# A planned kernel for hashed attention and two expert layers: wider zero products, a later start of a head's transposes, and a new planned order

## The chip, the cores and the metric

One core of one Trainium2 chip. The metric is the device time of one execution in microseconds; the median of several executions counts. The kernel before takes 838.75 us (three runs, 838.18 to 839.08).

## The reference

Only the numbers of the work matter here, and what depends on what.

```python
# q, k, v: (2, 8, 768, 64); proj: (64, 6)
bucket = sum over 6 bits of (x @ proj > 0) * 2**bit         # for q and for k
scores = where(q_bucket == k_bucket, q @ k.T / 8, -1e9)     # 16 heads of 768 x 768
attn   = softmax(scores);  y = attn @ v                     # -> x: (1536, 512)
g      = h * tanh(softplus(h)),  h = x @ w_in               # 512 -> 2048
x2     = g @ w_out                                          # 2048 -> 512
out    = ((x2 @ w1) * (x2 @ w2)) @ w3 @ w_out2              # 512 -> 1024 -> 1024 -> 512
```

## The kernel before, in words

Everything is computed in float32 accuracy: a float32 operand is split into a high and a low part in the type fp32r, and three products of the parts (`PASS`) stand for one. The sixteen heads are worked through one after the other. **A head** (`prep`, `scores`, `unit`, `values`, `norm`): its q and k are split and transposed on TensorE (L441, into a PSUM pair `s`), copied out by ScalarE as `qb` and `kb` (L447), the hash bits are products with `psel` (L472) and are compared on VectorE (L479, L484); then come six score tiles of 128 rows (L499, four products each, into `s`), each with its maximum on VectorE (L508) and its exponential on ScalarE (L511); the exponentials `E` are transposed on TensorE (L545, three to a bank `b`), copied out as `T` by ScalarE or VectorE (L400), and multiplied with v (L569). At the head's end the six sums are inverted (L522 to L524), transposed (L528), copied as `rt` (L530) and stored to `r_d`. There are two pairs `s` and four banks `b` in PSUM.

**Weights**: raw weights (8-byte numbers) are loaded by GpSimd's queue (L622), decoded by one ScalarE operation and three VectorE operations (L606 to L615, on 128x1024 elements), and stored again as `keep_...` (L640). Later SyncE's queue fetches them (L654), and they are split (L661, L663). The product of w3 and w_out2 (`wprod`, L694, L711) is computed beside the heads, and so is the whole chain of the first block of 512 tokens (`ff_first`: L775, L791, L886), whose input is scaled with rows of `r_d` (`x_split`, L742 to L762). Its banks are evicted by ScalarE or VectorE (L821, L851, L895, L897, L922). The two other blocks of 512 tokens follow (L775, L1133, L1160, L1188).

**The order** is made by a planner (`Plan`). Each step is a `P.op`: an engine (or two to choose from), an assumed duration, what it reads and writes, and a due time. `Plan.run` goes forward in its own time: it finds the engine on which a step can begin first, and of the steps that can begin there then takes the one that is due first. A value (`Val`) gets a buffer of its pool when the first step that names it begins, and a kind of value may hold at most `lim` buffers. What a step hands on counts as there after its duration, a latency (`LAT`, or its own `lat`) and `slack`. Each engine then runs its steps in this order and waits on semaphores, so an assumed duration sets the order alone, not the waiting. `CFG` has the due times' parameters, in units of one score tile, the most ScalarE-only `T` copies (`tc`, in score tiles), and the most banks that the first block's chain may hold (`F`).

**Zero products**: after planning, `Plan.fill` goes through the gaps that the plan leaves on TensorE (up to `fill`, 60 of the plan's microseconds), and puts products of zeros (`zeros`, L392) into a bank that is free then. Their number is the gap's length divided by an assumed duration of one.

Of the kernel before, what the change touches and what calls it, by code (L numbers as in the profile page):

```python
# [24 lines left out]
PASS = ((0, 0), (0, 1), (1, 0))  # L25

CFG = {
    "lag": 1.18,
    "prep": 8.06,
    "wp0": 16.01,  # L30
    "wp1": 51.97,
    "dec0": 47.99,
    "dec1": 88.63,
    "ff0": 56.0,
    "ff1": 102.69,
    "slack": 0.10,
    "k8": 12,
    "f4": 7,
    "hl": 3,
    "F": 3,  # L40
    "cold": 8.0,
    "fill": 60.0,
    "tc": 22,
}


# [34 lines left out]


class Plan:
    LAT = {"PE": 0.22, "DVE": 0.17, "ACT": 0.17, "POOL": 0.3, "SP": 2.3, "SWAP": 0.0}

    def __init__(self):
        self.units = []
# [58 lines left out]
    def fill(self, order):  # L146

        last = 0.0
        for u in [x for x in order if x.eng == "PE"]:
            a, b = last, u.start  # L150
            last = u.start + u.alts["PE"]
            if a > CFG["fill"]:
                break
            n = int((b - a - 0.15) / 0.06)
            if n < 4:
                continue
            for p in self.filler_pools:
                for i in range(len(p.bufs)):
                    if all(y <= a or x >= b + 0.1 for x, y in p.spans.get(i, [])):
                        f = Unit()  # L160
                        f.alts, f.eng, f.start, f.idx, f.name = {"PE": b - a - 0.1}, "PE", a + 0.01, -1, "zero"
                        f.fn = lambda p=p, i=i, n=n: self.filler(p.bufs[i], n)
                        order.append(f)
                        p.spans.setdefault(i, []).append((a, b))
                        break
                else:
                    continue
                break
# [118 lines left out]
def kernel(  # L287
# [14 lines left out]
    nc = tc.nc  # L302
# [86 lines left out]
    def zeros(t, n):  # L389
        t = t[:, 0] if len(t.shape) == 3 else t  # L390
        for _ in range(n):
            nc.tensor.matmul(t[:, 0:128], lhsT=zr, rhs=zr, start=True, stop=True)  # L392

    P.filler, P.filler_pools = zeros, (BP, SP_)
    P.free["PE"] = 1.3
# [25 lines left out]
    def prep(u, d0, step):  # L421

        def d(x):
            return d0 + x * step

        qb, kb, qa, ka = feat[u] = Val(QB, "f"), Val(KB, "f"), Val(QA, "f"), Val(KA, "f")
        for x, (nm, hi, fb) in enumerate((("q", 0, qb), ("k", 1, kb))):
            raw = raws.pop((u, nm))
            hl = Val(HL, "h")
            P.op(EITHER, (act(C * D, True), dve2(C * D)), lambda e, raw=raw, hl=hl, hi=hi: copy(e, hl()[:, :, hi, :], raw()),  # L430
                 r=[raw], w=[(hl, "hi")], due=d(x), name=f"sp{u}")
            P.op("DVE", dve(C * D), lambda raw=raw, hl=hl, hi=hi: nc.vector.tensor_sub(
                out=hl()[:, :, 1 - hi, :], in0=raw(), in1=hl()[:, :, hi, :]),
                r=[raw, (hl, "hi")], w=[(hl, "lo")], due=d(x), name=f"sp{u}")
            t = Val(SP_, "tq", 1)

            def tr(hl=hl, t=t):
                tt = t().bitcast(FR)
                for c in range(C):
                    a, i = divmod(c, CH)  # L440
                    nc.tensor.transpose(  # L441
                        tt[:, a, i * 128:(i + 1) * 128], hl()[:, c].rearrange("p s d -> p (s d)"), identr)

            P.op("PE", 6 * 0.082, tr, r=[hl], w=[t], due=d(x + 1), name=f"tq{u}")

            def fbc(t=t, fb=fb, nm=nm):
                nc.scalar.activation(  # L447
                    out=fb().rearrange("p (a n) -> p a n", a=2), in_=t()[:, :, 0:HS], func=AF.Copy,
                    scale=1.0 if nm == "q" else 1.0 / float(D) ** 0.5)

            P.op("ACT", act(S) + 0.01, fbc, r=[t], w=[fb], due=d(x + 1.3), name=f"fb{u}")
        xf = None
        if u > 1:
            xf = Val(XF, "x")
            for sl, fb, nm in ((slice(0, D), qb, "q"), (slice(D, 2 * D), kb, "k")):
                P.op("SP", 0.5, lambda sl=sl, fb=fb: nc.sync.dma_start(
                    out=xf()[sl].bitcast(F32), in_=fb()[sl].bitcast(F32)), r=[fb], w=[(xf, nm)], due=d(2.5), lat=2.0, name=f"xf{u}")
        P.op(EITHER, (act(S, True), dve2(S)), lambda e: copy(e, qa()[0:D], qb()[0:D]),
             r=[qb], w=[(qa, "x")], due=d(2.2), name=f"fa{u}")
        P.op(EITHER, (act(S, True), dve2(S)), lambda e: copy(e, ka()[0:D], kb()[D:2 * D]),  # L460
             r=[kb], w=[(ka, "x")], due=d(3.2), name=f"fa{u}")
        t = Val(SP_, "tq", 1)

        def bits(a):
            cols = slice(a * HS, (a + 1) * HS)
            ops = [(psel[:, 0, 0, :], qb()), (psel[:, 1, 0, :], kb())]
            if xf is None:
                ops += [(psel[:, 0, 1, :], qb()), (psel[:, 1, 1, :], kb())]
            else:
                ops += [(psel2, xf())]  # L470
            for n, (w, f) in enumerate(ops):
                nc.tensor.matmul(t()[:, a, 0:HS], lhsT=w, rhs=f[:, cols], start=(n == 0), stop=(n == len(ops) - 1))  # L472

        for a in range(2):
            P.op("PE", pe(HS, 4 if xf is None else 3), lambda a=a: bits(a),
                 r=[qb, kb, v_psel] + ([xf, v_psel2] if xf else []), w=[(t, a)], due=d(4), name=f"bits{u}")

        def cmp():
            nc.vector.tensor_scalar(  # L479
                out=qa()[D:128].rearrange("p (a n) -> p a n", a=2), in0=t()[D:128, :, 0:HS],  # L480
                scalar1=ccol[D:128, 1:2], scalar2=ccol[D:128, 0:1], op0=ALU.is_le, op1=ALU.mult)

        P.op("DVE", 0.99, cmp, r=[t, v_ccol], w=[(qa, "m")], due=d(4.3), name=f"cmp{u}")
        P.op("DVE", dve2(S), lambda: nc.vector.tensor_copy(out=ka()[D:KR], in_=qa()[96:96 + 2 * NB]),  # L484
             r=[(qa, "m")], w=[(ka, "m")], due=d(4.6), name=f"km{u}")
# [30 lines left out]
    def norm(u, due):  # L516
# [3 lines left out]
        def sc():  # L520
# [10 lines left out]
             due=due + 0.6, name=f"nr{u}")  # L531
        P.op("SP", 0.5, lambda: nc.sync.dma_start(
            out=r_d[h % 2, h // 2, b * S:(b + 1) * S].rearrange("(c p) -> c p", p=128), in_=rt()),
            r=[rt], w=[(v_rd, (u, ))], due=due + 0.7, lat=2.2, name=f"rd{u}")

    def n0_of(u, a):
        return u * C + a * CH
# [81 lines left out]
    def rawload(src, due, nm, after=()):  # L619
        raw = Val(K8, "raw", 2, I32)  # L620
        m = src.shape[1]
        P.op("POOL", 1.0, lambda: nc.gpsimd.dma_start(  # L622
            out=raw().rearrange("p (m n) -> p m n", m=m), in_=src), w=[raw], due=due, lat=8.0, name=nm + "l", after=after)
        return raw

    WSRC = {"wi": w_in, "wo": w_out, "wa": w1, "wb": w2}
# [7 lines left out]
    def decode_chunk(nm, j, due, waits=None):  # L634
        raw = rawload(chunk_src(nm, j), due - 1.5, f"{nm}{j}", after=late_gate + (waits or []))
        g = Val(F4, "g", 2)
        decode(raw, g, due, f"{nm}{j}")
        keep[nm, j] = dram.tile([128, 1024], F32, tag=f"{nm}{j}", name=f"keep_{nm}{j}")
        kept[nm, j] = Val()
        P.op("POOL", 1.0, lambda: nc.gpsimd.dma_start(out=keep[nm, j], in_=g()), r=[g], w=[kept[nm, j]],  # L640
             due=due + 0.4, lat=4.5, name=f"{nm}{j}s")

    hl_lim, ld_lim, fx_lim, late, fetched = [CFG["hl"]], [2], [1], [""], []

    def fetch(nm, j, due, ahead, after=()):

        after = list(after) + fetched[-1:]
        f, hl = Val(F4, "ld" + late[0], ld_lim[0]), Val(K8, "hl" + late[0], hl_lim[0], FR)
        if nm == "wp":
            src = wp_d[j * 256:(j + 1) * 256].rearrange("(f p) d -> p f d", p=128)  # L650
            P.op("SP", 0.5, lambda: nc.sync.dma_start(out=f().rearrange("p (f d) -> p f d", f=2), in_=src),
                 r=[(v_wp, 2 * j), (v_wp, 2 * j + 1)], w=[f], due=due - ahead - 1, lat=4.0, after=after, name=f"{nm}{j}ld")
        else:
            P.op("SP", 0.5, lambda: nc.sync.dma_start(out=f(), in_=keep[nm, j]), r=[kept[nm, j]], w=[f],  # L654
                 due=due - ahead - 1, lat=4.0, after=after, name=f"{nm}{j}ld")
        fetched.append(P.units[-1])
        split(f, hl, due - ahead)
        return hl
# [72 lines left out]
    def x_split(n, due, after=()):  # L731
# [3 lines left out]
        for kk in range(KD):  # L735
# [5 lines left out]
            for e in range(2):  # L741
                P.op("SP", 0.5, lambda e=e, kk=kk, rb=rb: nc.sync.dma_start(  # L742
                    out=rb()[e * D:(e + 1) * D], in_=r_d[e, kk, t0:t1].partition_broadcast(D)),
                    r=[(v_rd, (x, )) for x in us if x % 2 == e], w=[(f, ("r", e)), (xh, ("a", kk, e))], due=due, lat=2.3,
                    after=after, name=f"rb{n}")
            need = [(X[n], (x, a)) for x in us for a in range(2)
                    if (x // H) * S + a * HS < t1 and (x // H) * S + (a + 1) * HS > t0]
# [461 lines left out]
    OPS = {"h": b_h, "out": b_out, "x2": b_x2, "ab": b_ab, "o": b_o, "x": lambda n: x_split(n, clock[0] - 10, [P.units[-1]])}  # L1209
    for op, *a in step_list():  # L1210
        OPS[op](*a)
    global LAST
    LAST = P.run()
# [1 line left out]
_INS = ['q', 'k', 'v', 'proj', 'moe_w_in', 'moe_w_out', 'moe2_w1', 'moe2_w2', 'moe2_w3', 'moe2_w_out']  # L1215
_OUTS = [((1536, 512), 'float32')]
# [28 lines left out]
```

## Time and profile before

| what | value |
| --- | --- |
| median of 3 runs | 838.75 us (838.18 to 839.08) |
| the profiled execution, its own time | 839.55 us |
| its span, first to last instruction | 837.8 us |
| TensorE busy | 823.1 us (98%), 4198 products |
| VectorE busy | 551.3 us (66%) |
| ScalarE busy | 465.7 us (56%) |
| zero products (L392) | 272, of 128 columns |
| mean granted clock of TensorE | 0.998 |

The page of the profile gives busy times of the whole span, and 98% on TensorE contains zero products and stretched products as well. What the span is made of is read from the chain of waits (the work that ended last, followed back from the end), from busy times by stage, and from the groups of instructions by line. The clock column of a stretch reads 1.00 before the first record of the clock too; there the durations of equal products show the level.

### The profile page before, as it was taken

What the parts mean: (1) busy time and instruction counts of PE and PEld (TensorE: products, weight loads), DVE (VectorE), ACT (ScalarE), POOL (GpSimd) and SP (SyncE); (2) the same over time, 40 slices, a digit from 0 to 9 for tenths busy, and PEclk for the clock granted to TensorE, in tenths of its full rate; (3) what the DMA queues carried; (4) which work ended last, traced back from release to release, by engine and by line L of the source; (5) the groups of instructions that cost most, each with busy time, mean ns of one, the idle gap of its engine ahead of it and who ended that gap; (6) DMA issues with size and microseconds to landing.
All of it is one profiled execution on the core that took longest, in us unless ns stands there. A gap on an engine that the chain in (4) does not pass through costs nothing.

```text
span 837.8 us, 10922 instructions
## 1 busy us (share of the span) xinstructions
PE 823.1 (98%) x4198; PEld 637.1 (76%) x4198; DVE 551.3 (66%) x782; ACT 465.7 (56%) x735; POOL 42.5 (5%) x84
## 2 busy tenths in 40 slices
PE   9999999999989999999999999999999999999998
PEld 9977777777666766767777777888888888888886
DVE  3489878778889899989997566733644334332412
ACT  3379865666879978877675444633343333342311
POOL 3000000000101111111110000000000000000000
PEclk9999999999999999999999999999999999999999
DMA  7514433333956758667662203933212208300001
GB/s 271 222 36 152 139 112 103 111 92 115 286 178 209 256 176 275 243 217 268 217 205 72 83 6 133 407 125 104 79 69 88 102 1 317 110 26 1 1 0 51
DMA packets 40356, 118.47 MB, mean 141 GB/s; under 512 B 4496, under 2 KB 10992, under 8 KB 39280
## 3 DMA queue, kind: packets, MB, share of 16 engines
q1 hardware_dynamic: 27936, 67.31, 24.3%
q0 software_dynamic: 12224, 50.34, 17.5%
q8 instruction: 33, 0.54, 0.3%
q14 instruction: 19, 0.16, 0.1%
q10 hardware_dynamic: 144, 0.13, 0.0%
HBM read 94.37 MB, written 17.87 MB: 134 GB/s over the span
## 4 chain that ended last, share of the span: by engine, by line
PE 78%; DVE 12%; DMA 4%; issue 3%; ACT 3%; SPq 0%; DVEq 0%; ACTq 0%
PE s L1160 11%; PE b L1133 11%; PE s L775 11%; PE b L791 6%; PE b L569 6%; PE b L886 6%; PE b L1188 5%; PE s L499 5%; PE b L545 5%; PE b L711 4%; PE b L392 4%; DMA f<-r_d 3%; DVE st L508 2%; PE s L472 2%; PE b L775 2%
## 5 line engine op out<-in xcount | busy, mean ns | idle before, releaser
L663 DVE TENSOR_TENSOR k<-f,k 128x1024 fp32r<-128x1024 f32 x96 | 116.0, 1219 | 76.4 <-ACT k L661 76.2
L661 ACT CAST k<-f 128x1024 fp32r<-128x1024 f32 x96 | 99.2, 1047 | 20.5 <-DMA f<-keep_wo 7.8
L511 ACT ACTIVATE E<-s,st 128x768 f32<-128x768 f32 x96 | 86.8, 904 | 41.1 <-DVE st L508 40.0
L508 DVE TENSOR_REDUCE st<-s 128x1 f32<-128x768 f32 x96 | 90.9, 951 | 21.6 <-PE s L499 20.9
L400 ACT COPY T<-b 128x384 f32<-128x384 f32 x129 | 60.4, 483 | 60.1 <-PE b L545 59.8
L545 PE MATMUL b<-ident,E 128*128 128x128 f32 x576 | 93.1, 275 | 0.1
L545 PEld LDWEIGHTS b<-ident,E 128*128 128x128 f32 x576 | 71.0, 140 | 28.6 <-issue 9.0
L1160 PE MATMUL s<-k,k 128*128 128x512 f32 x384 | 91.2, 394 | 0.0
L1133 PE MATMUL b<-k,k 128*128 128x512 f32 x384 | 90.3, 393 | 0.0
L775 PE MATMUL s<-k,k 128*128 128x512 f32 x384 | 89.9, 391 | 0.0
L569 PE MATMUL b<-T,v 128*64 128x386 f32 (+1 forms) x384 | 85.2, 515 | 2.7 <-DVE T L400 2.7
L1160 PEld LDWEIGHTS s<-k,k 128*128 128x128 f32 x384 | 72.1, 188 | 16.8
L1133 PEld LDWEIGHTS b<-k,k 128*128 128x128 f32 x384 | 72.1, 188 | 16.5
L775 PEld LDWEIGHTS s<-k,k 128*128 128x128 f32 x384 | 72.1, 188 | 15.9
L791 PE MATMUL b<-k,k 128*128 128x512 f32 x288 | 81.0, 412 | 1.6 <-DVE k L851 1.6
L791 PEld LDWEIGHTS b<-k,k 128*128 128x128 f32 x288 | 51.3, 191 | 22.2 <-issue 9.6
L1111 ACT ACTIVATE f<-s 128x1024 f32<-128x1024 f32 x16 | 16.4, 1027 | 75.1 <-PE s L775 75.1
L1169 DVE TENSOR_TENSOR f<-s,f 128x512 f32<-128x512 f32 x16 | 11.1, 692 | 69.6 <-ACT f L1168 69.6
L499 PE MATMUL s<-kb,qb 128*128 128x384 f32 x192 | 53.2, 358 | 3.0 <-ACT E L511 2.7
L711 PE MATMUL b<-k,k 128*128 128x512 f32 x192 | 55.3, 413 | 0.0
L775 PE MATMUL b<-k,k 128*128 128x512 f32 x192 | 54.7, 410 | 0.5 <-ACT rt L530 0.5
L886 PE MATMUL b<-k,k 128*128 128x512 f32 x192 | 54.9, 411 | 0.0
(113 smaller groups left out, 1169.2 us busy)
## 6 DMA issues: line engine op xcount, KB each, us to landing
k<-in_moe_w_dram POOLq DMA_DIRECT2D x16, 1024.0 KB, 6.8
k<-in_moe_w_out_dram POOLq DMA_DIRECT2D x12, 1024.0 KB, 8.2
f<-keep_wi SPq DMA_DIRECT2D x24, 512.0 KB, 4.5
f<-keep_wo SPq DMA_DIRECT2D x24, 512.0 KB, 3.4
k<-in_moe_w_in_dram POOLq DMA_DIRECT2D x8, 1024.0 KB, 7.4
f<-keep_wa SPq DMA_DIRECT2D x12, 512.0 KB, 5.8
f<-keep_wb SPq DMA_DIRECT2D x12, 512.0 KB, 7.2
f<-wp_d SPq DMA_DIRECT2D x12, 512.0 KB, 3.7
```

The lines of the kernel that those rows point to most:

```text
L499: nc.tensor.matmul(t()[:, a, 0:HS], lhsT=l()[0:kk, i * 128:(i + 1) * 128], rhs=r()[0:kk, a * HS:(a + 1) * HS], start=(l is qb), stop=(l is ...
L508: P.op("DVE", 0.868, lambda: nc.vector.tensor_reduce(out=s()[:, 0, i:i + 1], in_=t()[:, :, 0:HS], axis=AX.XY, op=ALU.max, negate=True), r= ...
L545: nc.tensor.transpose(t()[:, ci * 128:(ci + 1) * 128], es[ci]()[:, kt * 128:(kt + 1) * 128], ident)
L569: nc.tensor.matmul(t()[x * D:(x + 1) * D, 0:n], lhsT=vs[u]()[:, 2 * j + x, :], rhs=fs[x]()[:, 0:n], start=(j == 0), stop=(j == CH - 1))
L661: P.op("ACT", act(1024, True), lambda: nc.scalar.copy(out=hl()[:, 0:1024], in_=f()), r=[f], w=[(hl, 0)], due=due, name="hi")
L663: P.op("DVE", dve(1024), lambda: nc.vector.tensor_sub(out=hl()[:, 1024:2048], in0=f(), in1=hl()[:, 0:1024]), r=[f, (hl, 0)], w=[(hl, 1)], ...
L711: nc.tensor.matmul(acc(), lhsT=hv()[:, ws, g_, :], rhs=wview(wo2[g_ // 2], 2)[:, rs, g_ % 2, :], start=(n == 0), stop=(n == 3 * GT - 1))
L775: nc.tensor.matmul(of(), lhsT=wview(w, KD)[:, ws, kk, (f % 2) * 128:(f % 2) * 128 + 128], rhs=kview(xhl[n][kk // 2], xs, kk), start=(m == ...
L791: nc.tensor.matmul(of(), lhsT=l(), rhs=rr(), start=(m == 0), stop=(m == len(ops) - 1))
L886: nc.tensor.matmul(t(), lhsT=wview(w, KD)[:, ws, kk, f2 * 128:f2 * 128 + 128], rhs=kview(x2[kk // 2], xs, kk), start=(kk == 0 and s == 0), ...
L1133: nc.tensor.matmul(t(), lhsT=wview(w, 2)[:, ws, f, dd * 128:(dd + 1) * 128], rhs=gv[:, gs, f, :], start=(j == 0 and f == 0 and s == 0), st ...
L1160: nc.tensor.matmul(t()[:, x, :], lhsT=wview(w, KD)[:, ws, kk, (f % 2) * 128:(f % 2) * 128 + 128], rhs=kview(xx[kk // 2], xs, kk), start=(k ...
```

## The change

Five things. Zero products have 512 columns instead of 128, and `fill` counts 0.43 us for one while the plan's time is under `cold` (8.0) and 0.235 us after, instead of 0.06 us; it fills gaps from one such product up. A head's transposes also name the buffer into which they are copied, so that they begin only when that buffer is free. The planner's latencies of transfers are longer. The first block's chain holds at most two banks instead of three. The due times are others (of their table two lines stand here). The last lines no longer keep the plan in a global name; that adds and removes no instruction.

```diff
-    "dec0": 47.99,
+    "dec0": 31.41,
...
-    "F": 3,
+    "F": 2,
...
-    LAT = {"PE": 0.22, "DVE": 0.17, "ACT": 0.17, "POOL": 0.3, "SP": 2.3, "SWAP": 0.0}
+    LAT = {"PE": 0.22, "DVE": 0.17, "ACT": 0.17, "POOL": 0.3, "SP": 3.2, "SWAP": 0.0}
...
-            n = int((b - a - 0.15) / 0.06)
-            if n < 4:
+            n = int((b - a - 0.1) / (0.43 if a < CFG["cold"] else 0.235))
+            if n < 1:
                 continue
...
-            nc.tensor.matmul(t[:, 0:128], lhsT=zr, rhs=zr, start=True, stop=True)
+            nc.tensor.matmul(t.rearrange("p (a n) -> p a n", a=4), lhsT=zr, rhs=zr[:, None, :].to_broadcast([128, 4, 128]),
+                             start=True, stop=True)
...
-            P.op("PE", 6 * 0.082, tr, r=[hl], w=[t], due=d(x + 1), name=f"tq{u}")
+            P.op("PE", 6 * 0.082, tr, r=[hl], w=[t, (fb, "t")], due=d(x + 1), name=f"tq{u}")
```

The longer latencies: the copies of `qb` and `kb` to `xf` 4.5 us (2.0 before), the store of `rt` 3.5 (2.2), a raw load 9.5 (8.0), the store of a decoded chunk 6.0 (4.5), a fetch of one 6.0 (4.0), the load of rows of `r_d` in `x_split` 6.0 (2.3).

In the changed file the lines after L392 have numbers one higher. Both programs have the same instructions on every engine but for the zero products (272 of 128 columns before, 36 of 512 now) and for copies that went from ScalarE to VectorE or back (13 more `T` copies on VectorE).

TensorE, at head 0's second to fourth score tile (`zr` zeros, `kb`/`qb` and `ka`/`qa` the two products of a score tile, `s` the PSUM pair). Before:

```order
L392 MATMUL b_69<-zr 128x128 x40
L499 MATMUL s_67<-kb_91,qb_89 128x384 x2
L499 MATMUL s_67<-ka_95,qa_93 128x384 x2
L392 MATMUL b_69<-zr 128x128 x40
L499 MATMUL s_67<-kb_91,qb_89 128x384 x2
```

and now:

```order
L392 MATMUL b_69<-zr 128x512 x7
L500 MATMUL s_68<-kb_91,qb_89 128x384 x2
L500 MATMUL s_68<-ka_95,qa_93 128x384 x2
L500 MATMUL s_67<-kb_91,qb_89 128x384 x2
L500 MATMUL s_67<-ka_95,qa_93 128x384 x2
L392 MATMUL b_69<-zr 128x512 x7
L500 MATMUL s_68<-kb_91,qb_89 128x384 x2
```

Forty zero products between two score tiles have become seven or none, and the score tiles now alternate between both pairs `s`. Head 1's hash bits (L472, eight products), which stood after head 0's last score tile, now stand four before and four after its first one. From the program's begin to head 1's first score tile there stand zero products in runs of 25, 28, 6, 15, 40, 40, 51, 4, 22, 21 and 6 before, and of 3, 5, 1, 5, 7 and 7 now; later runs are one of 14 before, and of 3 and 5 now.

GpSimd's queue, from its tenth weight load before and its ninth now (`in_moe_w` of 2048 columns is w3 for the product of weights, `in_moe_w_in` is w_in, `keep_wi` the store of a decoded chunk of it). Before:

```order
L622 DMA k_979<-in_moe_w_dram 128x2048
L622 DMA k_1059<-in_moe_w_dram 128x2048
L622 DMA k_1207<-in_moe_w_dram 128x2048
L622 DMA k_1354<-in_moe_w_in_dram 128x4x512
L622 DMA k_1508<-in_moe_w_in_dram 128x4x512
L622 DMA k_1670<-in_moe_w_in_dram 128x4x512
L640 DMA keep_wi_132<-f_1871 128x1024
```

Now:

```order
L623 DMA k_646<-in_moe_w_in_dram 128x4x512
L623 DMA k_810<-in_moe_w_dram 128x2048
L623 DMA k_949<-in_moe_w_in_dram 128x4x512
L641 DMA keep_wi_132<-f_1025 128x1024
L623 DMA k_1113<-in_moe_w_dram 128x2048
L623 DMA k_1123<-in_moe_w_in_dram 128x4x512
L641 DMA keep_wi_133<-f_1170 128x1024
L623 DMA k_1240<-in_moe_w_in_dram 128x4x512
L623 DMA k_1307<-in_moe_w_dram 128x2048
```

The first layer's weights now come between those of the product of weights, and are decoded earlier. In VectorE's order 14 of the 36 decodes stood before head 7's inverse (L524), and 19 do now; between that one and head 13's it was 20, and is 15.

## Rows read from the trace of the kernel before

**Rows 1.** The page: span, and TensorE's busy time (share) xinstructions.

```profile
span 837.8 us, 10922 instructions
PE 823.1 (98%) x4198; PEld 637.1 (76%) x4198; DVE 551.3 (66%) x782; ACT 465.7 (56%) x735; POOL 42.5 (5%) x84
```

**Rows 2.** Chain of waits, 0 to 60 us: shares by line; then start us, us, what.

```profile
by line: PE b L392 57.1%; PE s L499 7.5%; PE s L472 6.9%; PE s L441 5.6%; PE b L569 3.9%; PE b L545 3.5%; DVE st L508 3.1%; DVE k L612 2.0%; DVE f L615 1.9%; DVE qa L479 1.8%; issue 1.0%; DVE hlqk L432 0.9%; DVE ka L400 0.9%; DVE ka L484 0.
...
1.05 5.59 PE b L392 x25
...
12.96 1.52 PE s L441 x12
...
15.78 0.76 PE s L441 x6
16.54 2.69 PE s L472 x8
...
22.00 0.78 PE s L499 x4
22.78 4.42 PE b L392 x40
...
39.53 1.64 PE b L545 x15
41.17 1.45 PE b L569 x8
...
50.74 1.46 PE s L472 x8
```

**Rows 3.** Timeline, ScalarE and TensorE: first exponential, head 1's first score tile.

```profile
24.64 0.90 ACT L511 ACTIVATE E<-s,st 128x768 f32<-128x768 f32 x1 [3.14 <-DVE st L508]
...
54.48 0.60 PE L499 MATMUL s<-kb,qb 128*128 128x384 f32 x2
```

**Rows 4.** Groups by line, whole span: xcount | busy us, mean ns of one.

```profile
L511 ACT ACTIVATE E<-s,st 128x768 f32<-128x768 f32 x96 | 86.8, 904 | 41.1 <-DVE st L508 40.0
L400 ACT COPY T<-b 128x384 f32<-128x384 f32 x129 | 60.4, 483 | 60.1 <-PE b L545 59.8
L612 DVE SCALAR_TENSOR_TENSOR k<-k 128x1024 int32<-128x1024 int32 x36 | 44.3, 1231 | 0.5
L606 ACT ACTIVATE f<-k 128x1024 f32<-128x1024 f32 x36 | 41.4, 1151 | 0.0
L392 PEld LDWEIGHTS b<-zr 128*128 128x128 f32 x272 | 37.7, 222 | 2.3 <-issue 1.2 <-DVE zr L385 1.1
L511 ACT ACTIVATION_READ_ACCUMULATOR E<-s,st 128x1 f32 x96 | 18.8, 196 | 0.0
```

**Rows 5.** Stages between heads' inverses: PE, PEld, DVE, ACT, POOL busy, clock, DMA.

```profile
54.00:74.00 20.00, 19.28 (x126) 13.91 (x125) 19.36 (x29) 15.67 (x33) 1.06 (x2) 1.00 0.46 146
119.00:142.00 23.00, 23.00 (x142) 17.18 (x142) 18.47 (x32) 14.57 (x31) 1.29 (x2) 1.00 0.44 130
216.00:248.00 32.00, 27.96 (x155) 19.32 (x151) 27.79 (x45) 24.76 (x46) 2.91 (x4) 1.00 0.75 238
277.00:316.00 39.00, 37.72 (x192) 27.24 (x191) 35.49 (x52) 32.70 (x49) 5.61 (x8) 1.00 0.63 205
353.00:392.00 39.00, 37.44 (x188) 27.31 (x187) 35.31 (x51) 29.89 (x43) 6.17 (x8) 0.96 0.64 214
```

**Rows 6.** Chain of waits, whole span: start us, us, what.

```profile
62.52 1.71 PE b L392 x14
...
218.50 6.08 DMA f<-r_d
...
282.17 9.37 DMA f<-r_d
...
589.85 22.13 PE b L1133 x96
```

**Rows 7.** Waits: engine line waited for: us in total, times, longest us.

```profile
PE b L791 <- DVE k L851: 1.6, 1, 1.6
```

More of the change, by code (lines that the diff above doesn't have):

```diff
@@ L27 @@
 CFG = {
[L28 to L31, printed above, removed]
-    "dec0": 47.99,
-    "dec1": 88.63,
-    "ff0": 56.0,
-    "ff1": 102.69,
+    "lag": 1.46,
+    "prep": 8.48,
+    "wp0": 18.09,
+    "wp1": 51.13,
+    "dec0": 31.41,
+    "dec1": 107.42,
+    "ff0": 56.1,
+    "ff1": 105.58,
     "slack": 0.10,
@@ L39 @@
     "hl": 3,
-    "F": 3,
+    "F": 2,
     "cold": 8.0,
     "fill": 60.0,
-    "tc": 22,
+    "tc": 11,
 }
@@ L456, in prep @@
                 P.op("SP", 0.5, lambda sl=sl, fb=fb: nc.sync.dma_start(
-                    out=xf()[sl].bitcast(F32), in_=fb()[sl].bitcast(F32)), r=[fb], w=[(xf, nm)], due=d(2.5), lat=2.0, name=f"xf{u}")
+                    out=xf()[sl].bitcast(F32), in_=fb()[sl].bitcast(F32)), r=[fb], w=[(xf, nm)], due=d(2.5), lat=4.5, name=f"xf{u}")
         P.op(EITHER, (act(S, True), dve2(S)), lambda e: copy(e, qa()[0:D], qb()[0:D]),
@@ L533, in norm @@
             out=r_d[h % 2, h // 2, b * S:(b + 1) * S].rearrange("(c p) -> c p", p=128), in_=rt()),
-            r=[rt], w=[(v_rd, (u, ))], due=due + 0.7, lat=2.2, name=f"rd{u}")
+            r=[rt], w=[(v_rd, (u, ))], due=due + 0.7, lat=3.5, name=f"rd{u}")
     def n0_of(u, a):
@@ L622, in rawload @@
         P.op("POOL", 1.0, lambda: nc.gpsimd.dma_start(
-            out=raw().rearrange("p (m n) -> p m n", m=m), in_=src), w=[raw], due=due, lat=8.0, name=nm + "l", after=after)
+            out=raw().rearrange("p (m n) -> p m n", m=m), in_=src), w=[raw], due=due, lat=9.5, name=nm + "l", after=after)
         return raw
@@ L640, in decode_chunk @@
         P.op("POOL", 1.0, lambda: nc.gpsimd.dma_start(out=keep[nm, j], in_=g()), r=[g], w=[kept[nm, j]],
-             due=due + 0.4, lat=4.5, name=f"{nm}{j}s")
+             due=due + 0.4, lat=6.0, name=f"{nm}{j}s")
     hl_lim, ld_lim, fx_lim, late, fetched = [CFG["hl"]], [2], [1], [""], []
@@ L651, in fetch @@
             P.op("SP", 0.5, lambda: nc.sync.dma_start(out=f().rearrange("p (f d) -> p f d", f=2), in_=src),
-                 r=[(v_wp, 2 * j), (v_wp, 2 * j + 1)], w=[f], due=due - ahead - 1, lat=4.0, after=after, name=f"{nm}{j}ld")
+                 r=[(v_wp, 2 * j), (v_wp, 2 * j + 1)], w=[f], due=due - ahead - 1, lat=6.0, after=after, name=f"{nm}{j}ld")
         else:
             P.op("SP", 0.5, lambda: nc.sync.dma_start(out=f(), in_=keep[nm, j]), r=[kept[nm, j]], w=[f],
-                 due=due - ahead - 1, lat=4.0, after=after, name=f"{nm}{j}ld")
+                 due=due - ahead - 1, lat=6.0, after=after, name=f"{nm}{j}ld")
         fetched.append(P.units[-1])
@@ L743, in x_split @@
                     out=rb()[e * D:(e + 1) * D], in_=r_d[e, kk, t0:t1].partition_broadcast(D)),
-                    r=[(v_rd, (x, )) for x in us if x % 2 == e], w=[(f, ("r", e)), (xh, ("a", kk, e))], due=due, lat=2.3,
+                    r=[(v_rd, (x, )) for x in us if x % 2 == e], w=[(f, ("r", e)), (xh, ("a", kk, e))], due=due, lat=6.0,
                     after=after, name=f"rb{n}")
@@ L1211 @@
         OPS[op](*a)
-    global LAST
-    LAST = P.run()
+    P.run()
 _INS = ['q', 'k', 'v', 'proj', 'moe_w_in', 'moe_w_out', 'moe2_w1', 'moe2_w2', 'moe2_w3', 'moe2_w_out']
```

## The prediction

> **What bounds the kernel now.** I read the page first, then the busy times by stage, then the chain of waits, and the groups by line for prices. The page says that TensorE is busy 98% of the span [rows 1], so at first sight only TensorE work can be saved. The chain tells what this work is. In the first 60 us it runs through zero products for 57.1% [rows 2], that is 34.3 us, and once more later for 1.71 us [rows 6]: 36.0 us together, in eleven of the twelve runs of zeros. They were to fill gaps, but they do not fit them. Forty of them take 4.42 us [rows 2], 0.11 us each, where the planner counted 0.06; in the first run 25 take 5.59 us, 0.22 each. So each run ends after the work that it was to bridge, and head 0's score tiles stand some 5 us apart (22.00, then behind a run that ends at 27.2). ScalarE shows it from the other side: it idles 3.14 us before the first exponential [rows 3], for a tile that TensorE had ready late. Head 1's first score tile begins only at 54.48 us [rows 3].
>
> After 54 us another picture. Up to 216 us TensorE has nearly no idle time, and VectorE has room while the product of weights runs beside the heads: 18.47 of 23 us in the stage from 119 us, the others there being like it [rows 5]. From 216 to 392 us TensorE idles 4.04 us, 1.28 us and 1.56 us in the three stages shown [rows 5], and in the last the clock falls to a mean of 0.96 of 39 us, which is 1.6 us more at the level of 1.2 GHz. In these stages the chain waits for rows of `r_d` to land, 6.08 and 9.37 us at once [rows 6], where the planner counted 2.3, and VectorE is busy over nine tenths of two of them [rows 5], so it has no room to catch up. The three stages hold 8.5 us of lost TensorE time. The two later blocks are products without a gap (96 of 512 columns in 22.13 us [rows 6], 0.231 each), which the change leaves as they are.
>
> **The zero products, term 1.** 272 of 128 columns go, 36 of 512 come, 14 ahead of the first score tile and 22 after. No row shows a zero product of 512 columns. From below, its price is that of any product of 512 columns, 0.231 us [rows 6]; at the low clock it is that of the hash bits, eight of 384 columns in 2.69 us [rows 2], so 0.45 us for 512. (That these run at 1.2 GHz is seen from the eight at 50.74 us, which take 1.46.) From above, it goes per column as the small ones do: 0.44 us, and 0.89 at the low clock. I take the lower price, because the small ones pay for something that a long one hides: their weight loads keep the load path busy for 37.7 us [rows 4], as long as the products themselves, whereas products of 512 columns come at 0.231 although each loads weights too. So the zeros cost 14 x 0.45 + 22 x 0.231 = 11.4 us (upper price: 22.2) where 36.0 stood on the path: **-24.6 us** (-13.8 by the upper price).
>
> That only counts if TensorE really is what sets the beginning. So I walk it, with the rows of group 2. Zeros begin at 1.05. Now come 3 zeros (1.35), two transposes for constants (0.25 at the pace of the twelve at 12.96 us), 5 zeros (2.25), twelve transposes (1.52), 1 zero (0.45), six transposes (0.76), eight hash products (2.69), six transposes (0.76), 5 zeros (2.25) and four hash products of head 1 (1.35): the first score tile at 14.7 us, not 22.00. From there to head 1's first score tile TensorE has six score tiles (0.78 each), four hash products (0.73), 14 zeros (3.23), 24 transposes of `E` (0.109), six of `q` (at most 0.76) and six products with v (0.18): 12.9 us, so 27.6 us. ScalarE's share: its first exponential 2.6 us after the score tile as before (24.64 against 22.00), then six exponentials (0.904 + 0.196), six `T` copies (0.483) and one decode (1.151) [rows 4], 10.7 us: 28.0 us. Both bounds agree, and the later one holds: 28 us against 54.48, 26.5 us earlier. Of this, 6 + 6 products that before had behind them (0.7 + 1.1) and the 8 zeros still to come (1.8) go off, and the later run of 1.71 us that vanishes comes on: -24.6 again. The cover of the zeros is thus real waiting for VectorE and ScalarE in about 1 us of it only.
>
> **The waits for transfers, term 2.** The rows of `r_d` now count as landing 6.0 us after their issue instead of 2.3, so VectorE's multiplication that reads them (L748) stands later in its queue, with other work ahead. The decodes moved too: five of 36 now stand before head 7's inverse where VectorE had room, and not in the five heads after. One holds VectorE for some 3 us (three operations, the dearest 1.23 us [rows 4]), so about 15 us leave a stretch in which it was full. Bounds: none of the 8.5 us goes, or all. I take 6, since the chain names the transfer in each of the three stages: **-6 us**. What is late next there is VectorE itself.
>
> **What comes back, term 3.** (a) The decodes that moved up. VectorE was busy 18.47 of 23 us [rows 5]; one decode more makes it 21.5, two more 24.6, which is over. Some of these heads will wait a little: 0 to 5 us, I take +1. (b) Two banks instead of three for the first block. A bank of six products is refilled after 1.4 us, in which the eviction of the bank before must come through VectorE's queue. With three banks TensorE waited for it once, 1.6 us [rows 7], behind a transfer that was late. Between banks the order still has a head's transposes or products. 0 to +4 us, I take +0.5. (c) The transposes that wait for their copies' buffer: nothing new is issued; they hold no pair `s` while the copy cannot be made, and are issued later in exchange. ScalarE's queue covers either, so 0. (d) Copies that changed engines: thirteen `T` copies at 0.48 us off ScalarE, onto a VectorE that has room early and little late; in (a).
>
> Sum: -24.6 - 6 + 1.5 = -29.1 us. The profiled execution took 839.55 us with a span of 837.8; its span would be 808.7. The median of the runs lies 0.8 us under that execution, so 838.75 - 29.1 = 809.65: I say **809.5 us**.
>
> **Rivals.**
> 1. *The wide zeros are dear.* Each would take 0.44 us (0.89 at the low clock), by column as the small ones. Then term 1 is -13.8, and the time 820 us. For it: the only zero products that the trace has cost this per column. Against it: the load path, above. Chance 0.06.
> 2. *VectorE takes over.* With the zeros gone VectorE and ScalarE have 25 us less for the same work, VectorE 551.3 us in all, most of it before 500 us [rows 1]. Between 54 and 74 us it is busy 19.36 of 20 us already [rows 5]. If each of the eight heads from the first inverse on took 1.5 us longer and none of the 6 us were won, the time would be 838.75 - 24.6 + 12 = 826 us. For it: 13 more copies and five decodes come just there. Against it: ahead of head 1 both engines waited for TensorE behind its zeros (ScalarE 3.14 us in one place [rows 3]), and that time is now theirs. Chance 0.13.
> 3. *Two banks are too few*, the case on the other side. All of the first block's 80 banks (16 of h, 32 of x2, 16 of ab, 16 of o) pass through two. If the wait for VectorE's eviction (one operation of 1.2 us in front, as L612 [rows 4]) came at half the banks, 40 x 1.2 = 48 us would come back: 838.75 - 29.1 + 48 = 858 us. It decides from 0.36 us a bank on. For it: rows 7 show the wait already with three. Against it: that was one wait of 80 banks. Chance 0.04.
> 4. *The clock falls without the zeros.* Zeros kept TensorE at work; the stage from 353 us shows what waiting does (mean 0.96 [rows 5]). If TensorE ran heads 0 to 2 at 1.2 GHz, some 15 us of products a head at up to twice their time, between 10 and 15 us would come back in each that VectorE does not cover; with two such heads beyond VectorE's 19 us each, about 20 us: 829 us. Against it: from 54 to 74 us TensorE has transposes, products with v and waits, and only 14 zeros, at a clock of 1.00 [rows 5]. Chance 0.03. The Trainium skill has a rule that speaks for this rival: by "TensorE: Matmul & The Clock Gate", Part 4 (PE-mode transpose), TensorE's full clock does not engage for transposes. By that rule a beginning of transposes with few zeros would lose the clock and end near rival 4; the row from 54 us disagrees as far as transposes among other products go, and shows no stretch of transposes alone.
> 5. *The change does nothing*: 838.75 us, if each removed zero turned into waiting for VectorE or ScalarE. ScalarE's 3.14 us of idle time [rows 3] speaks against it. Chance 0.02.
>
> **How the numbers follow.** The forecast has 0.72. Its own range: at best all of the 8.5 us, the clock with it, and another 6 us of VectorE's 15 go (838.75 - 24.6 - 14.5 = 799.7); at worst nothing of them goes and term 3 reaches +4 (818). Rival 1 lies at 820, rival 2 at 826. The range 799 to 822 takes in the forecast and rival 1 and leaves out rivals 2 to 5, 0.22, of which the better half of rival 2's cases is inside. A measurement of this kernel tells about 0.2% (1.7 us) from no change. Slower by more: rival 3 and a worse rival 4, 0.05. Within: rival 5, 0.02. Faster: 0.93.
>
> **What would show it.** Right: 36 zero products at 0.23 us (0.43 to 0.45 at the low clock) and some 11 us of them on the chain; the first score tile near 15 us, head 1's first near 28, head 0's inverse near 30 instead of 54; TensorE's idle time from head 8 on under 4 us, with the waits for `r_d` off the chain. Wrong: zeros of 0.44 us (rival 1), heads 1 to 7 longer than before with VectorE full (rival 2), waits of L791 and L886 for L851, L897 or L922 (rival 3), a clock under 1.00 between 20 and 80 us (rival 4).

## The result, and the profile after

The changed kernel takes 812.0 us (median of 4 runs, 810.3 to 813.94) against 838.91 us of the kernel before beside it; the ratio is 0.9679, 95% interval 0.9655 to 0.9703. Forecast were 809.5 us, in a range of 799 to 822. The profiled execution took 812.21 us with a span of 810.4.

The page of the changed kernel, span and busy times; [rows 1] before:

```profile
span 810.4 us, 10455 instructions
PE 796.4 (98%) x3962; PEld 606.3 (75%) x3962; DVE 555.0 (68%) x792; ACT 459.9 (57%) x725; POOL 40.8 (5%) x84
```

TensorE's busy time falls by 26.7 us, nearly the whole gain, and its share stays at 98%. The begin is where it went. The changed kernel's chain of waits, 0 to 60 us, with start, us, what (beside [rows 2]):

```profile
5.95 6.10 DMA rw<-in_q_dram
12.05 0.03 issue
...
13.13 1.10 DVE qa L480
14.27 0.98 PE s L473 x4
15.26 0.70 PE s L500 x4
15.96 1.22 PE s L473 x4
17.18 2.66 PE b L392 x7
19.83 1.42 PE s L500 x8
21.26 1.62 PE b L392 x7
```

Zeros stand in it with 7.1% of the 60 us instead of 57.1%. In their place the chain begins with something that was not there: a load of q, and VectorE behind it. The zero products, busy time over two stretches (PE, PEld, clock, DMA):

```profile
0.00:60.00 60.00, 12.90 (x36) 8.40 (x36) 0.97 0.60 208
60.00:810.40 750.40, 0.00 (x0) 0.00 (x0) 1.00 0.42 141
```

Head 1's first score tile, the last line of [rows 3] now, in TensorE's timeline; and the first exponential in ScalarE's:

```profile
30.14 0.62 PE L500 MATMUL s<-kb,qb 128*128 128x384 f32 x2
...
17.05 0.90 ACT L512 ACTIVATE E<-s,st 128x768 f32<-128x768 f32 x1 [5.42 <-DVE st L509]
```

Stages between heads' inverses, the columns of [rows 5]: to head 0's inverse, to head 1's, then heads 5, 8, 10 and 12.

```profile
0.00:32.00 32.00, 26.85 (x140) 21.71 (x140) 19.58 (x37) 18.50 (x32) 6.77 (x31) 0.95 0.78 284
32.00:51.10 19.10, 18.33 (x107) 12.36 (x108) 18.79 (x28) 17.58 (x35) 0.48 (x1) 1.00 0.35 106
...
121.20:147.40 26.20, 25.94 (x150) 18.79 (x149) 23.05 (x33) 22.29 (x41) 3.05 (x5) 1.00 0.76 242
...
200.30:220.40 20.10, 19.86 (x119) 13.73 (x118) 19.10 (x33) 15.22 (x32) 2.04 (x3) 1.00 0.83 272
...
250.30:288.70 38.40, 36.88 (x191) 26.50 (x189) 35.34 (x55) 31.09 (x44) 3.77 (x6) 1.00 0.50 162
...
325.50:359.10 33.60, 33.60 (x177) 24.98 (x176) 33.05 (x49) 26.06 (x39) 3.89 (x6) 1.00 0.75 250
```

Head 8, where TensorE idled 4 us before, has 0.24 us of it now, and head 12 neither idles nor loses the clock. From head 8 to head 15 TensorE idles 2.8 us in all, 8.6 before. The rows of `r_d` are off the chain: the only transfer left among its named pieces is the load of q above.

For all kernels below I use two numbers from TensorE's timeline of the profiled execution: the start of the third transposed inverse (L528; "heads 0 to 2"), and from there to the start of the last product ("rest"). Later stages are often the same to 0.1 us in two kernels, so these tell apart what a median cannot.

| kernel | median us | ratio to before, 95% interval | heads 0 to 2 | rest |
| --- | --- | --- | --- | --- |
| before | 838.91 | | 93.9 | 739.6 |
| changed | 812.0 | 0.9679, 0.9655 to 0.9703 | 72.4 | 733.7 |
| zeros alone on before | 822.87 | 0.9806, 0.9769 to 0.9844 | 80.2 | 738.3 |
| claim alone on before | 826.74 | 0.9860, 0.9843 to 0.9877 | 83.2 | 736.6 |
| zeros and claim on before | 814.41 | 0.9708, 0.9694 to 0.9723 | 71.2 | 736.9 |
| changed, old zeros | 823.6 | 0.9810, 0.9784 to 0.9835 | 83.8 | 733.6 |
| changed, no zeros | 814.45 | 0.9708, 0.9679 to 0.9738 | 73.4 | 733.8 |
| changed, no claim | 821.8 | 0.9792, 0.9754 to 0.9829 | 85.2 | 730.1 |
| changed, old latencies | 822.25 | 0.9797, 0.9752 to 0.9842 | 68.7 | 747.4 |
| changed, old latency of r_d rows | 812.48 | 0.9691, 0.9674 to 0.9707 | 72.6 | 733.5 |
| changed, old due times | 848.93 | 1.0123, 1.0108 to 1.0138 | 74.4 | 769.2 |
| changed, three banks | 814.29 | 0.9695, 0.9648 to 0.9742 | 74.1 | 735.3 |
| changed, split of head 2 later | 808.82 | 0.9638, 0.9602 to 0.9674 | 69.0 | 733.5 |

### The profile page after: what moved, and what is told of

Same layout as the page of the kernel before. It is cut to its first block, busy times and chain, and to the rows that moved or that the text cites. A ratio compares the mean times of both kernels' runs of the same rounds, so it can differ in the third digit from the quotient of the medians.

```text
span 810.4 us, 10455 instructions
## 1 busy us (share of the span) xinstructions
PE 796.4 (98%) x3962; PEld 606.3 (75%) x3962; DVE 555.0 (68%) x792; ACT 459.9 (57%) x725; POOL 40.8 (5%) x84
## 4 chain that ended last, share of the span: by engine, by line
PE 73%; DVE 19%; ACT 3%; issue 3%; DMA 1%; SPq 1%; DVEq 0%
PE s L1161 11%; PE b L1134 11%; PE s L776 11%; PE b L887 6%; PE b L1189 5%; PE b L792 5%; PE b L570 5%; PE s L500 4%; PE b L712 4%; PE b L546 4%; DVE st L509 4%; PE b L776 3%; DVE k L613 2%; DVE f L616 2%; DVE k L664 2%
## 5 line engine op out<-in xcount | busy, mean ns | idle before, releaser
L546 PE MATMUL b<-ident,E 128*128 128x128 f32 x576 | 95.2, 276 | 0.5 <-DVE T L401 0.2
L1134 PE MATMUL b<-k,k 128*128 128x512 f32 x384 | 90.2, 393 | 0.0
L570 PE MATMUL b<-T,v 128*64 128x386 f32 (+1 forms) x384 | 83.4, 512 | 0.0
L792 PE MATMUL b<-k,k 128*128 128x512 f32 x288 | 78.9, 405 | 0.0
L401 ACT COPY T<-b 128x384 f32<-128x384 f32 x116 | 55.0, 482 | 41.2 <-PE b L546 39.0
L500 PE MATMUL s<-kb,qb 128*128 128x384 f32 x192 | 55.6, 370 | 0.3 <-ACT E L512 0.3
L712 PE MATMUL b<-k,k 128*128 128x512 f32 x192 | 54.1, 408 | 0.5 <-DVE k L703 0.5
L776 PE MATMUL b<-k,k 128*128 128x512 f32 x192 | 53.0, 406 | 1.1 <-DVE T L401 0.7
L1169 ACT COPY f<-s 128x512 f32<-128x512 f32 x16 | 9.4, 587 | 77.2 <-PE s L1161 77.2
```

The source lines that it names most:

```text
L500: nc.tensor.matmul(t()[:, a, 0:HS], lhsT=l()[0:kk, i * 128:(i + 1) * 128], rhs=r()[0:kk, a * HS:(a + 1) * HS], start=(l is qb), stop=(l is ...
L546: nc.tensor.transpose(t()[:, ci * 128:(ci + 1) * 128], es[ci]()[:, kt * 128:(kt + 1) * 128], ident)
L570: nc.tensor.matmul(t()[x * D:(x + 1) * D, 0:n], lhsT=vs[u]()[:, 2 * j + x, :], rhs=fs[x]()[:, 0:n], start=(j == 0), stop=(j == CH - 1))
L712: nc.tensor.matmul(acc(), lhsT=hv()[:, ws, g_, :], rhs=wview(wo2[g_ // 2], 2)[:, rs, g_ % 2, :], start=(n == 0), stop=(n == 3 * GT - 1))
L776: nc.tensor.matmul(of(), lhsT=wview(w, KD)[:, ws, kk, (f % 2) * 128:(f % 2) * 128 + 128], rhs=kview(xhl[n][kk // 2], xs, kk), start=(m == ...
L792: nc.tensor.matmul(of(), lhsT=l(), rhs=rr(), start=(m == 0), stop=(m == len(ops) - 1))
```

## Experiments on the zero products

**The zeros alone on the kernel before**, its old order kept: `fill` and `zeros` as in the change, nothing else.

```diff
-            n = int((b - a - 0.15) / 0.06)
-            if n < 4:
+            n = int((b - a - 0.1) / (0.43 if a < CFG["cold"] else 0.235))
+            if n < 1:
```

> The kernel before with the zero products of 512 columns and their count alone; its order, latencies and banks are the old ones. The old gaps are longer, so it has 60 zero products. My theory (each costs what any product of 512 columns does, 0.23 us, and 0.45 at the low clock, and what they no longer take is won in full): 11 x 0.45 + 49 x 0.231 = 16.3 us where 36.0 stood, so 19.7 us less, 819 us; the rest of the change's gain is then the new order's. Rival (the gain is the new order, whose score tiles stand closer): under 8 us less, 831 us or more. Rival (zeros go by column, 0.44 us): 11 x 0.89 + 49 x 0.44 = 31 us, 834 us.

It takes 822.87 us, 16.2 us less than the kernel before beside it (839.07). The wide zeros do not go by column, and the gain is not the new order's alone: the first theory holds, with 3.5 us less than it said, and alone the zeros give more than half of the whole gain. Its chain now holds a load of q from 7.09 us on, 8.15 us long, which the expectation did not count. The old order without overfull gaps still needs 40.5 us to head 0's inverse, where the changed kernel needs 32.3. So the gaps themselves were longer there. The edit changes the zeros' width and their count together. No kernel was run with zeros of 128 columns counted at the 0.11 and 0.22 us that they take, so how much of the 16.2 us needs the width is not shown.

**The old zeros in the new order**: the same lines of the changed kernel set back.

> The changed kernel with the old zero products of 128 columns, counted as before at 0.06 us: 176 of them in the new order's gaps. My theory: 88 stand ahead of the first score tile at 0.22 us (19.4 us) and 88 behind at 0.11 (9.7), 29 us where 11.4 stand now; about 3 us of it lies in a wait that TensorE has there anyway. So 13 to 17 us slower than the changed kernel, about 826. Rival (the new order alone makes the gain): within 3 us of the changed kernel.

It takes 823.6 us, 11.6 us more than the changed kernel, somewhat less than the 13 to 17 that were expected. The rest of the program is untouched (733.6 us), and no transfer stands on its chain. The new order without the new zeros wins 15.5 us on the kernel before, the new zeros without the new order 16.2, both together 26.9: they share some 5 us.

What the zeros do to the clock shows here as well. The chain of this kernel, eight hash products at the begin, and under it busy time of the same eight in the changed kernel (PE, PEld, clock, DMA):

```profile
18.89 2.69 PE s L472 x8
```

```profile
7.80:9.30 1.50, 1.48 (x8) 1.33 (x8) 1.00 0.94 261
```

With 60 zeros of 128 columns and ten more ahead of them they run at 1.2 GHz at 19 us; with nine of 512 columns they run at 2.4 GHz at 8 us. The clock record of the changed kernel has the full clock from 5.7 us, that of this one from 22.7.

**No zeros**: `for _ in range(0)` in the changed kernel's `zeros`.

> The changed kernel without any zero product. Theory that zeros only cost: up to 8 us faster, 804 us. Theory that the clock needs them: TensorE stays at 1.2 GHz beyond 20 us, the hash products take 0.34 us instead of 0.18 throughout the begin; 3 to 10 us slower, 815 to 822 us. Mine: gains and losses of some 3 us each, 809 to 814 us.

It takes 814.45 us; head 0's inverse begins at 32.8 us instead of 32.3, heads 0 to 2 end 1.0 us later. The clock rises at 16.8 us instead of 5.7, and it is low again in two stretches that the changed kernel runs at full clock (PE, PEld, DVE, ACT, POOL, clock, DMA):

```profile
20.00:26.80 6.80, 6.14 (x21) 4.55 (x21) 2.35 (x3) 4.60 (x10) 0.00 (x0) 0.52 1.03 416
...
50.70:54.10 3.40, 3.32 (x17) 3.24 (x18) 3.17 (x8) 3.35 (x9) 0.00 (x0) 0.53 0.04 8
```

In the first, TensorE had idled half of the 3.5 us before. So the zeros earn a little more than they cost, 1 us by the stages and 2.4 by the medians; the runs' ranges overlap slightly (810.3 to 813.94 and 813.28 to 815.69), and so do the intervals of the two ratios, so a gain is likely and not certain.

## Experiments on the transposes' claim

**The claim taken out** of the changed kernel, and the rest planned anew:

```diff
-            P.op("PE", 6 * 0.082, tr, r=[hl], w=[t, (fb, "t")], due=d(x + 1), name=f"tq{u}")
+            P.op("PE", 6 * 0.082, tr, r=[hl], w=[t], due=d(x + 1), name=f"tq{u}")
```

> The changed kernel, planned anew without the transposes' claim on their copies' buffer. My theory (term 3c): nothing, within 3 us, which is what another order alone may do. Rival (a pair s held by waiting transposes holds up score tiles, 2 us a head): 5 us slower or more.

821.8 us: 9.8 us slower, and head 0's inverse 7.8 us later, head 1's 17.9. In TensorE's order all six score tiles of head 0 now go to `s_67`, as in the kernel before. The chain of this kernel:

```profile
15.71 3.75 PE b L392 x10
19.46 0.71 PE s L500 x4
20.17 2.30 PE b L392 x10
22.47 0.82 PE s L500 x4
23.29 2.32 PE b L392 x10
25.61 0.81 PE s L500 x4
```

These gaps of ten zero products are real: the next score tile begins 0.15 us after the exponential of the one before ends. ScalarE's and TensorE's timelines of this kernel:

```profile
21.26 0.90 ACT L512 ACTIVATE E<-s,st 128x768 f32<-128x768 f32 x1 [2.55 <-DVE st L509]
```

```profile
22.31 0.62 PE L500 MATMUL s<-kb,qb 128*128 128x384 f32 x2
```

The reason lies with head 2. Its transposed q sits in the other pair from 14 us on (six products of L442 there), and its copy (`qb_89<-s_68`) stands on ScalarE behind five exponentials of head 0, since it overwrites the `qb` that head 0's last score tile still reads. So the score tiles go one after the other through a single pair, product, maximum, exponential, next product. The claim lets the transposes wait outside of PSUM.

**The zeros and the claim on the kernel before**, and **the claim alone**: the line above put into the kernel with the new zeros, and into the kernel before.

> The kernel before with the new zero products and the transposes' claim on their copies' buffer; old due times, old latencies, three banks. My new theory (one of the two pairs s is held by head 2's transposes in the kernel before, so head 0's score tiles follow one another through a single pair; the claim frees it, and the planner then leaves few gaps): score tiles alternate between both pairs, head 0's inverse near 29 us instead of 40.2 with the zeros alone, the waits for r_d stay; 10 us faster than the zeros alone, 812 us. Old theory (the claim is worth nothing): 820 us or more.

814.41 us, 8.5 us less than the zeros alone, and head 0's inverse at 28.9 us: near the 10 us and the 29 us that were expected. The planner leaves 34 zero products where it left 60. The waits for `r_d` stay, as said; the chain names them with 5.53, 4.50 and 3.85 us between 196 and 224 us. Heads 0 to 2 take 71.2 us, a little less than in the changed kernel: the begin is won by these two edits alone.

> The kernel before with the claim alone; old zero products, 165 of them in the gaps that it leaves (272 before). New theory: 107 zero products at 0.11 us less and the pair freed: 11 to 13 us faster than the kernel before, 826 us, head 0's inverse near 42. Old theory (worth nothing): within 3 us of the kernel before.

826.74 us, 11.8 us less than the kernel before, as expected; head 0's inverse is at 40.9 us (near 42 expected).

## Experiments on latencies, due times and banks

**Old latencies**: `LAT` and the six `lat` of the diff set back in the changed kernel, planned anew.

> The changed kernel, planned anew with all transfer latencies of the kernel before. My theory (term 2: 6 of the 8.5 us that TensorE lost between heads 8 and 12 went because the planner now counts what transfers take): VectorE waits for rows of r_d again, the chain names them, TensorE idles 6 us more from head 8 on, 818 us. Rival (the fewer decodes from head 8 on did it, not the latencies): within 2 us of the changed kernel, no r_d on the chain.

822.25 us, 10 us slower although the begin is 3.7 us shorter; the rest is 13.7 us longer. The chain, and the stage of head 8 (from 193.4 to 236.0 us):

```profile
194.28 5.69 PE b L712 x24
...
204.03 11.53 DMA f<-r_d
...
218.75 1.28 PE s L500 x4
```

```profile
193.40:236.00 42.60, 35.93 (x185) 26.57 (x185) 27.98 (x48) 23.83 (x44) 4.04 (x6) 0.88 0.58 171
```

VectorE stands behind a load of rows, ScalarE's exponentials behind VectorE, TensorE idles 6.7 us, and the clock is at 1.2 GHz for 10.2 us after.

**The old latency for these rows alone** (`lat=2.3` instead of 6.0 in `x_split`):

> The changed kernel with the old latency (2.3 us) for the rows of r_d alone. Theory (it is these rows whose latency mattered): VectorE waits for them again at head 8, up to 11 us in the chain, the clock falls, 7 us or more slower, 820 us. Rival (another latency, or several, made the old-latency kernel slow): within 3 us of the changed kernel.

812.48 us, the same as the changed kernel; the expectation was wrong. A wait of 4.37 us for the rows comes back into the chain at 207.6 us, TensorE idles 2.4 us at head 8 instead of 0.2, and the heads after win as much. So the rows' own latency does not carry the gain; which of the other latencies does, or whether it takes several, was not separated.

**Old due times** in the changed kernel (the old table, with two banks):

> The changed kernel planned with the old due times; new zeros, claim, latencies, two banks. Theory: the begin is as in the changed kernel (head 0's inverse near 32); the decodes stand late again (20 between head 7's and head 13's inverse), so VectorE is full there, 3 to 8 us slower, 817 us. Rival (the due times are worth nothing beside the latencies): within 2 us of the changed kernel.

848.93 us, slower than the kernel before, by much more than either theory said. Heads 9 to 14 take 20 to 27 us instead of 30 to 38, because the first block's chain falls behind them: 145 us of the program, with 566 of the chain's products, then lie between head 14's inverse and head 15's. TensorE idles 37.4 us in all (14.0 in the changed kernel), and its clock falls five times from 236 to 346 us. My reading, which no run tests by itself, is that the longer latencies put the chain's fetches off and the old due times do not pull them back. What the runs show is that these latencies pay with the new due times and not with the old ones (814.41 us with the old latencies, due times and three banks).

**Three banks** (`F` of 3 in the changed kernel, planned anew):

> The changed kernel, planned anew with three banks for the first block's chain (F of 3). My theory (term 3b): two banks cost 0 to 4 us, so this is 0 to 2 us faster than the changed kernel, or up to 3 us slower by the other order that a new plan makes anywhere. Rival 3 (each bank pays): over 5 us faster.

814.29 us; the difference to the changed kernel is inside its intervals. TensorE's waits for L852 are as short with two banks (0.9 us) as with three (1.1 in three places).

## Experiments on the new wait at the begin

VectorE's timeline of the changed kernel shows where the load of q comes in:

```profile
12.15 0.36 DVE L401 CAST hlqk<-rw 128x384 fp32r<-128x384 f32 x1 [3.23 <-DMA rw<-in_q_dram]
12.54 0.56 DVE L433 TENSOR_TENSOR hlqk<-rw,hlqk 128x384 fp32r<-128x384 f32 x1
13.13 1.08 DVE L480 TENSOR_SCALAR qa<-s,ccol 64x768 fp32r<-64x768 f32 x1
```

Head 2's split stands in VectorE's queue ahead of head 0's comparison (L480), whose eight hash products were done at 9.3 us. The load was issued at 5.95 us, when GpSimd's queue had begun with weights of 1 MB each, and took 6.1 us. TensorE waits 3.1 us, and its clock is low from 15.9 to 19.3 us. A first attempt to put this right was no fair test: it moved head 2's split behind head 1's comparison, and two loads that overwrite what the split reads stayed ahead of it, so head 2 is computed from head 4's q and k and waits for their loads. It takes 816.74 us.

> The changed kernel with one edit in VectorE's order: head 2's split, which waits 3.2 us for the load of q, stands behind head 1's comparison instead of ahead of head 0's. My theory: head 0's comparison begins near 9.4 us instead of 13.13, TensorE does not idle 3.1 us at the hash products, and its clock does not fall at 15.7 us; 4 to 6 us faster than the changed kernel, about 807. Rival (ScalarE and VectorE set the pace of the first heads, so an earlier begin is lost by head 2): under 1.5 us.

The second attempt moves the two loads as well, in the planned order, just before the steps are issued:

```diff
+        early = [u for u in order if u.name == "sp2"]
+        k0 = [u for u in order if u.name == "km1"]
+        if early and k0:
+            at = order.index(k0[0])
+            moved = [u for u in early if order.index(u) < at]
+            moved += [u for u in order[:at] if u.name in ("loadq4", "loadk4")]
+            order = [u for u in order if u not in moved]
+            at = order.index(k0[0]) + 1
+            order[at:at] = moved
```

> The changed kernel with head 2's split behind head 1's comparison in VectorE's order, and the two loads that overwrite what it reads issued behind it. My theory: head 0's comparison begins near 9.4 us instead of 13.13, TensorE does not idle 3.1 us at the hash products, and its clock does not fall at 15.7 us; 4 to 6 us faster than the changed kernel, about 807. Rival (VectorE and ScalarE set the pace of the first heads, so an earlier begin is lost by head 2): under 1.5 us.

VectorE's timeline of this kernel:

```profile
9.49 1.09 DVE L489 TENSOR_SCALAR qa<-s,ccol 64x768 fp32r<-64x768 f32 x1 [0.66 <-PE s L482]
```

The comparison begins at 9.49 us, head 0's inverse at 28.9 instead of 32.3, and the stages of the heads after are the same to 0.1 us. It takes 808.82 us (808.63 to 809.28); each of its runs is under each of the changed kernel's. This version beats both kernels. It wins 3.2 us and not the 4 to 6 that were expected: 3.4 us of begin, and the low clock of the changed kernel had stood over zeros for the most part.

## Why the prediction was right, and where it was not

- **Term 1, the zeros (-24.6 us): the size was right to 3 us, the reason given for it in part.** Heads 0 to 2 take 21.5 us less. The missing 3 are the wait for q, which the walk along TensorE's order did not see, because it looked at what TensorE and ScalarE do and not at what stands ahead of the comparison on VectorE: the first score tile came at 15.26 us (14.7 forecast), head 1's first at 30.14 (28.0). Without that wait (the last kernel of the table) the begin is 24.9 us shorter, 0.3 us from the forecast. That it comes so close is partly luck: there the first score tile comes at 11.86 us, 2.8 us ahead of the walk, and head 1's first at 26.77, only 1.2 us ahead of it. The walk's terms for TensorE between the two add up to 13.1 us, not 12.9; ScalarE's bound was the later one, so the 28 us do not change.
- **The price of a wide zero was right**: seven take 1.62 us in the chain at full clock, 0.231 us each, and five take 2.28 us at the low one (from 2.78 us on), 0.46 each. That the low clock would last up to the first score tile was wrong, it rose at 5.7 us; what this won fell into the new wait.
- **"The cover of the zeros is thus real waiting ... in about 1 us of it only" is the step that failed.** It is true of the changed order, where the walk was made. In the old order the gaps were real, and long, because one pair `s` was held; the zeros overfilled them. The zeros alone win 16.2 us, and the claim 8.5 more.
- **Term 3 (c), the claim at 0, was mis-sized**: 8.5 us beside the new zeros, 11.8 alone, 9.8 out of the changed kernel. The alternation of the pairs stood in the order's rows ahead of the prediction, which made nothing of it. The sum came out because the changed order, whose 36 zeros were priced and walked, already contains the claim's effect (60 zeros without it on the old order, 34 with it); the shares did not.
- **Terms 2, 3 (a) and 3 (b), -4.5 us together: the rest fell by 5.9 us (739.6 to 733.7), but not by these terms alone.** With the zeros and the claim on the kernel before, whose latencies, due times and banks are the old ones, it is 736.9, so 2.7 us go without these terms; the kernel before had lost its clock for 3.4 us (at 370.9 us), and that kernel did not. About 3.2 us are left for them, and 2.4 us by the medians (814.41 to 812.0), where the runs' ranges overlap. The waits for `r_d` are off the chain, as forecast. That VectorE's reading of these rows, counted 6.0 us late, does it, fell with its own experiment; the latencies as a set are worth 10 us beside the new due times. The first block's chain now ends later behind the heads (from head 15's inverse to the last product 344.3 us, before 334.5) and the heads are that much lighter, a shift that term 3 did not price. Two banks cost nothing that was measured.
- **Rival 4** was right in kind and wrong in size: after its first rise the clock fell once with few zeros, for 3.4 us, and three times as long without any, which with the zeros' own cost set against it comes to 1 to 2.4 us. In the changed kernel it stays full from 19.3 us on, through transposes among other products; no stretch of transposes alone in this trace is longer than 1.7 us. The Trainium skill ("TensorE: Matmul & The Clock Gate", Part 4) says that the full clock does not engage for transposes; this trace, with transposes among other products throughout, neither bears that out nor speaks against it.
- **Rivals 1, 2, 3 and 5 did not come**, though one sign of rival 2 did: heads 1 to 7 take 168.3 us, 162.2 before, with VectorE busy 84 to 98% of each. But TensorE idles at most 0.54 us in each of them. Heads 3 to 7 hold 171 products of the weights' product (L712) instead of 153: work that came forward, not waits.

## What to carry to other kernels

A gap that a filler covers should first be asked why it is there: here a buffer taken by a step whose next step could not yet run was worth 8.5 us beside the 16.2 of filler of the right length. Let a step claim the buffer it will be drained into before it takes a scarce one. When an order is planned from assumed times, change the times and the priorities together, and look in every in-order queue for a step that waits on a transfer ahead of one that is urgent.

## What was not expected of the hardware

The clock rose at 5.7 us in the changed kernel, after eight zero products of 512 columns and eight transposes. With zeros of 128 columns it rose at 22.7 us, after 73 of them, 26 transposes and eight hash products (old zeros in the new order), and at 19.4 us in the kernel before, after 59 zeros. Without any zeros it rose at 16.8 us, after transposes, hash products and the first score tile.

Loads of 192 KB took very different times at the begin. In the kernel before a load of k that was issued at 8.53 us, 1.1 us ahead of the first load of weights, landed after 2.4 us. Loads of q that were issued within 0.1 us of the first load of weights took 6.10 us in the changed kernel and 3.99 us in the one without zeros; with the zeros alone, where q was issued 1.0 us behind it, it took 8.15 us. That the weights hold them up is likely, but no run moves the weights alone.
